# Turning x, q and h into columns with 32x32 turns on VectorE in place of one-column matmuls, in a decode kernel on one core

## The chip, the cores and the metric

One core of one Trainium2 chip. The metric is the device time of one execution in microseconds. It is about 1.8 us longer than the span of the profile, which runs from the first to the last instruction.

Words used below: PE is TensorE, DVE is VectorE, ACT is ScalarE, POOL is GpSimd, SP is the engine that issues the big loads. "big" is the name of the three rotating 8 MB buffers for loads. K0 and V0 are the first pieces of the two caches, K1 and V1 the next. "w12" is w1 and w2 in one load. psq and psh are the accumulators of the matmuls with wq and with w3, and stand for these stages; ps is that of w12, and psB gathers the row that is returned. xT is x as a column, hT the same of h. A "turn" is VectorE's transpose of each 32x32 block. "fetch" is a transfer of a block of instructions. Times of DMA packets count from the same zero as the timelines, the first instruction of the program.

## The reference, cut to what matters

```python
xn = layernorm(x)                                # x: 1 x 1024
q  = xn @ wq                                     # 32 heads of 128
o  = softmax(q @ k_cache.T * 128**-0.5) @ v_cache  # 4 kv heads, 65536 keys: 134 MB of cache
a  = o @ wo
h  = gelu(layernorm(x1) @ w3) @ w4               # x1: the residual of the small mixer w1, w2
return x + a + mlp                               # 1 x 1024
```

One token is decoded, so nearly all of the work is to read the caches and the weights once: 170 MB.

## The kernel before

The loads go through three buffers. A load is issued when the buffer three loads earlier has been released, and a release is the end of the compute on it:

```python
stream = ["wq", "w3", "w12"]
for u in range(NU): stream += [("K", u), ("V", u)]     # wo ahead of the last V, w4 at the end
def pump(self):
    while self.next < len(stream) and self.held < SLOTS:   # SLOTS = 3
        self.load(...)
def done(self, it): self.held -= 1; self.pump()
```

The three places where a row has to become a column, each done with one-column matmuls (cuts marked):

```python
x_row = ogpool.tile([1, D], BF16, ...)
nc.scalar.dma_start(out=x_row[:], in_=A_x[0, 0:1, :])
...
for c in range(DC):                               # x: 8 matmuls
    nc.tensor.matmul(px[:, c:c + 1], lhsT=x_row[0:1, c::DC], rhs=pick4[0:1, 0:1], ...)
...
def row_matmul(acc, rep, cols, n_slices):         # q and h: slices of 512 columns, 4 in
    for c in range(DC):                           # parallel in 4 column groups of PE
        for i in range(2):
            for q in range((n_slices + 1 - i) // 2):
                nc.tensor.matmul(acc[32*q:32*q+32, i, :], lhsT=rep[:, c, :], rhs=cols(c, 2*q+i), ...)
...
for h in range(8):                                # q: 8 matmuls; h: 8 more like them
    nc.tensor.matmul(pq[:, 4, :]..., lhsT=q_row[:, h // 4, ...], rhs=pick4[:], ...)
```

The four column groups hold 32 equal rows each, since the left operand repeats one vector 32 times.

Of the kernel before, what the change touches and what calls it, by code (L numbers as in the profile page):

```python
# [8 lines left out]
BF16 = mybir.dt.bfloat16  # L9
F32 = mybir.dt.float32  # L10
ACTF = mybir.ActivationFunctionType
# [4 lines left out]
P = 128  # L16
# [36 lines left out]
def kernel(  # L53
# [14 lines left out]
    nc = tc.nc  # L68
    nc.at_finalize(keep_loaded_weights)
    D = A_x.shape[-1]  # L70
    S = A_x.shape[1]
    HKV = A_k_cache.shape[1]
# [4 lines left out]
    DC = D // P  # L77
    FC = F // P
# [8 lines left out]
    const = ctx.enter_context(tc.tile_pool(name="const", bufs=1))  # L87
    small = ctx.enter_context(tc.tile_pool(name="small", bufs=1))
    big = ctx.enter_context(tc.tile_pool(name="big", bufs=SLOTS))
    ppool = ctx.enter_context(tc.tile_pool(name="psb", bufs=1))  # L90
    ogpool = ctx.enter_context(tc.tile_pool(name="og", bufs=2))
    ps_S = ctx.enter_context(tc.tile_pool(name="psS", bufs=1, space=bass.MemoryType.PSUM))
    ps_O = ctx.enter_context(tc.tile_pool(name="psO", bufs=1, space=bass.MemoryType.PSUM))
    ps_M = ctx.enter_context(tc.tile_pool(name="psM", bufs=2, space=bass.MemoryType.PSUM))
# [53 lines left out]

    st = Stream()

    x_row = ogpool.tile([1, D], BF16, name="x_row", tag="og")
    nc.scalar.dma_start(out=x_row[:], in_=A_x[0, 0:1, :])
    st.pump()

    ident_f = const.tile([P, P], F32, name="ident_f")
# [4 lines left out]
    nc.gpsimd.memset(ones_f[:], 1.0)  # L160
    warm_act = const.tile([P, 1], F32, name="warm_act")
    nc.scalar.activation(out=warm_act[:], in_=eps_t[:], func=ACTF.Sqrt)
    pick4 = const.tile([P, 4], BF16, name="pick4")
    nc.gpsimd.tensor_copy(out=pick4[:], in_=ident_f[:, ::32])

    spread = ogpool.tile([P, 4, P], BF16, name="spread", tag="og")
    for b in range(2):
        nc.gpsimd.tensor_copy(
            out=spread[:, 2 * b:2 * b + 2, :].rearrange("p r (a i) -> p r a i", a=4),
            in_=ident_f[:, 64 * b:64 * b + 64].rearrange("p (i r) -> p r i", r=2).unsqueeze(2).to_broadcast([P, 2, 4, 32]))  # L170
# [9 lines left out]
        nc.tensor.matmul(psB[32 * j:32 * j + lhsT.shape[1], :], lhsT=lhsT, rhs=rhs, start=start, stop=False,  # L180
                         tile_position=(0, 32 * j), skip_group_check=True)

    px = ps_M.tile([P, 512], F32, name="pm_x", tag="pm")
    for c in range(DC):
        nc.tensor.matmul(px[:, c:c + 1], lhsT=x_row[0:1, c::DC], rhs=pick4[0:1, 0:1], start=True, stop=True)
    xT = const.tile([P, DC], F32, name="xT")
    nc.vector.tensor_copy(out=xT[:], in_=px[:, 0:DC])

    def layernorm(src, tag):
        rowsum = const.tile([P, 1], F32, name=f"ln_rowsum_{tag}", tag="ln_rowsum")  # L190
# [22 lines left out]
    xn, xn_rep, negmean1, rstd1 = layernorm(xT, "a")  # L213
    _, xn2_rep, _, _ = layernorm(xn, "b")
# [14 lines left out]
                          in_=sel8[:].unsqueeze(2).to_broadcast([P, 8, 16]))  # L229

    ln_s1 = const.tile([P, 1], F32, name="ln_s1")
    nc.vector.tensor_scalar(out=ln_s1[:], in0=rstd1[:], scalar1=1.0, scalar2=None, op0=ALU.add)
    ln_s2 = const.tile([P, 1], F32, name="ln_s2")
    nc.vector.tensor_tensor(out=ln_s2[:], in0=negmean1[:], in1=rstd1[:], op=ALU.mult)
    accx = ppool.tile([1, D], F32, name="accx", tag="p")
    nc.vector.tensor_scalar(out=accx[:], in0=x_row[:], scalar1=ln_s1[0:1, 0:1], scalar2=ln_s2[0:1, 0:1],
                            op0=ALU.mult, op1=ALU.add)
    for j in range(2):
        row_acc(j, ident_f[0:1, 0:32], accx[0:1, 512 * j:512 * (j + 1)], start=True)

    def row_matmul(acc, rep, cols, n_slices):
        for c in range(DC):
            for i in range(2):
                for q in range((n_slices + 1 - i) // 2):
                    nc.tensor.matmul(acc[32 * q:32 * q + 32, i, :], lhsT=rep[:, c, :], rhs=cols(c, 2 * q + i),  # L245
                                     start=(c == 0), stop=(c == DC - 1),
                                     tile_position=(0, 32 * q), skip_group_check=True)

    qx = const.tile([P, 4, 8 * HKV], BF16, name="qx")

    def compute_wq():
        wt = st.tiles["wq"][:].rearrange("p (c n) -> p c n", c=DC)
        psq = ps_S.tile([P, SUBS, 512], F32, name="psq", tag="sc")
        row_matmul(psq, xn_rep, lambda c, s: wt[:, c, 512 * s:512 * (s + 1)], 8)
        st.done("wq")
        q_row = ppool.tile([P, 2, 512], BF16, name="q_row", tag="p")
        nc.vector.tensor_copy(out=q_row[:, 0, :], in_=psq[:, 0, :])  # L257
        nc.scalar.copy(out=q_row[:, 1, :], in_=psq[:, 1, :])
        pq = ps_M.tile([P, 5, 8 * HKV], F32, name="pm_q", tag="pm")
        for h in range(8):  # L260
            nc.tensor.matmul(pq[:, 4, :].rearrange("p (g h) -> p g h", h=8)[:, :, h],
                             lhsT=q_row[:, h // 4, P * (h % 4):P * (h % 4 + 1)], rhs=pick4[:], start=True, stop=True)
        qT = small.tile([P, 8 * HKV], BF16, name="qT")
        nc.vector.tensor_copy(out=qT[:], in_=pq[:, 4, :])
        for x in range(4):
            nc.tensor.matmul(pq[:, x, :], lhsT=spread[:, x, :], rhs=qT[:], start=True, stop=True)
        nc.vector.tensor_copy(out=qx[:], in_=pq[:, 0:4, :])

    def place_queries(g):
        for a in range(4):  # L270
# [5 lines left out]
    hT = const.tile([P, FC], BF16, name="hT")  # L276

    def compute_w3():
        wt = st.tiles["w3"][:, 0:DC * F].rearrange("p (c m k) -> p c k m", c=DC, k=FC)
        psh = ps_S.tile([P, SUBS, 512], F32, name="psh", tag="sc")  # L280
        row_matmul(psh, xn2_rep, lambda c, s: wt[:, c, 4 * s:4 * s + 4, :], 7)
        st.done("w3")
        h_rows = ppool.tile([P, 2, 512], BF16, name="h_rows", tag="p")
        nc.vector.memset(h_rows[96:128, 1, :], 0.0)
        nc.scalar.activation(out=h_rows[:, 0, :], in_=psh[:, 0, :], func=ACTF.Gelu_apprx_tanh)
        nc.scalar.activation(out=h_rows[0:96, 1, :], in_=psh[0:96, 1, :], func=ACTF.Gelu_apprx_tanh)
        ph = ps_M.tile([P, 8, 4], F32, name="pm_h", tag="pm")
        for ik in range(8):
            nc.tensor.matmul(ph[:, ik, :], lhsT=h_rows[:, ik // 4, P * (ik % 4):P * (ik % 4 + 1)], rhs=pick4[:],  # L289
                             start=True, stop=True)  # L290
        nc.vector.tensor_copy(out=hT[:, 0:24].rearrange("p (q ik) -> p ik q", q=3), in_=ph[:, :, 0:3])  # L291
        nc.vector.tensor_copy(out=hT[:, 24:28], in_=ph[:, 0:4, 3])

    def compute_w12():
        wt = st.tiles["w12"][:, 0:2 * DC * D].rearrange("p (w c n) -> p w c n", w=2, c=DC)
# [130 lines left out]
    def compute_w4(lo, hi):  # L426
        wt = st.tiles["w4"]
        for c in range(lo, hi):
            for j in range(2):
                row_acc(j, hT[:, c:c + 1], wt[:, D * c + 512 * j:D * c + 512 * (j + 1)])  # L430

    compute_wq()
    compute_w3()
    compute_w12()
    for u in range(NU - 1):
# [4 lines left out]
    for g in range(HKV - 1):  # L440
# [11 lines left out]
                        in_=out_t[:].rearrange("(a b) n -> a b n", b=32)[:, 0, :])  # L452
# [29 lines left out]
```

## Time and profile before

| | before |
|---|---|
| time, median of the first 3 runs | 402.9 us (402.86 to 404.4) |
| span of the profiled run | 402.5 us |
| moved over the span | 170.03 MB, mean 422 GB/s |
| PE, DVE busy | 59%, 51% |

The profiled run is 404.32 us (from result.json of the run).

From the page of the kernel before: engine, busy microseconds, share of the span; the load totals; the instruction queue with its packets, megabytes and share; the chain of waits by engine.

```profile
span 402.5 us, 2599 instructions
PE 235.8 (59%) x1364; PEld 45.9 (11%) x878; DVE 204.7 (51%) x150; ACT 27.4 (7%) x35; POOL 5.5 (1%) x29
...
DMA packets 4576, 170.03 MB, mean 422 GB/s; under 512 B 467, under 2 KB 469, under 8 KB 982
...
q8 instruction: 9, 0.15, 0.1%
...
DMA 47%; PE 22%; DVE 14%; ACT 2%; issue 1%; DVEq 0%; ACTq 0%
```

The chain of waits gives PE and DVE over a third of the span. It would be a mistake to take that as what they cost. The chain walks back from one event to what released it, and a load that was released late still had other loads ahead of it in the queue. The timeline shows that. Its columns are start, duration, engine and line, operation, output and input, count, and in brackets the idle time before it and what ended it.

```profile
0.73 0.37 SPq L128 DMA_DIRECT2D big<-in_A_wq_dram  x1
0.74 0.53 ACTq L152 DMA_DIRECT2D x_row<-in_A_x_dram  x1
...
2.30 0.66 PE L185 MATMUL pm_x<-pick,x_row 1*128 1x1 bf16 x8 [2.30 <-DMA x_row<-in_A_x_dram]
...
22.64 5.39 PE L245 MATMUL psq<-big,ln_rep_a 128*32 128x512 bf16 x64 [11.09 <-DMA big<-in_A_wq_dram]
...
28.07 0.33 SPq L147 DMA_DIRECT2D big<-in_A_k_cache_dram  x1
...
39.57 14.17 PE L245 MATMUL psh<-big,ln_rep_b 128*32 128x512 bf16 x56 [9.34 <-DMA big<-in_B_w_dram]
...
53.77 0.33 SPq L147 DMA_DIRECT2D big<-in_A_v_cache_dram  x1
...
63.50 0.33 SPq L147 DMA_DIRECT2D big<-in_A_k_cache_dram  x1
...
70.28 8.77 DVE L322 STREAM_TRANSPOSE big<-big 128x4096 f32<-128x4096 f32 x2 [13.48 <-DMA big<-in_A_k_cache_dram]
...
396.23 0.99 PE L180 MATMUL psB<-big,hT 128*1 128x512 bf16 x6 [0.44 <-DMA big<-in_B_w_dram]
398.99 0.38 PE L180 MATMUL psB<-big,hT 128*1 128x512 bf16 x2 [1.76 <-DMA big<-in_B_w_dram]
```

K0 is issued at 28.07 while w3 and w12 are still under way. V0 is issued at 53.77 and K0 lands only at 70.28. So the queue always holds something, and what happens between 2 and 64 us should be free to come many microseconds later before a DMA engine is idle.

### The profile page before, as it was taken

What the parts mean: (1) busy time and instruction counts of PE and PEld (TensorE: products, weight loads), DVE (VectorE), ACT (ScalarE), POOL (GpSimd) and SP (SyncE); (2) the same over time, 40 slices, a digit from 0 to 9 for tenths busy, and PEclk for the clock granted to TensorE, in tenths of its full rate; (3) what the DMA queues carried; (4) which work ended last, traced back from release to release, by engine and by line L of the source; (5) the groups of instructions that cost most, each with busy time, mean ns of one, the idle gap of its engine ahead of it and who ended that gap; (6) DMA issues with size and microseconds to landing.
All of it is one profiled execution on the core that took longest, in us unless ns stands there. A gap on an engine that the chain in (4) does not pass through costs nothing.

```text
span 402.5 us, 2599 instructions
## 1 busy us (share of the span) xinstructions
PE 235.8 (59%) x1364; PEld 45.9 (11%) x878; DVE 204.7 (51%) x150; ACT 27.4 (7%) x35; POOL 5.5 (1%) x29
## 2 busy tenths in 40 slices
PE   5160973591579238743975195439354925694983
PEld 2010110000100110010002010100020102010220
DVE  3010000974196569634953895279449750965040
ACT  1000021003000200020002000200200020002000
POOL 2000000000000000000000000000000000000000
PEclk9996888696769787956795689669875976598999
DMA  9989999999999999999999999999999998999893
GB/s 397 436 382 421 443 423 462 469 417 417 418 423 462 462 406 423 417 436 451 456 417 417 430 438 430 469 417 417 423 444 423 469 423 378 430 457 449 381 417 142
DMA packets 4576, 170.03 MB, mean 422 GB/s; under 512 B 467, under 2 KB 469, under 8 KB 982
## 3 DMA queue, kind: packets, MB, share of 16 engines
q1 hardware_dynamic: 4560, 169.87, 98.0%
q8 instruction: 9, 0.15, 0.1%
q10 hardware_dynamic: 6, 0.00, 0.0%
q14 instruction: 1, 0.01, 0.0%
HBM read 169.87 MB, written 0.00 MB: 422 GB/s over the span
## 4 chain that ended last, share of the span: by engine, by line
DMA 47%; PE 22%; DVE 14%; ACT 2%; issue 1%; DVEq 0%; ACTq 0%
DMA big<-in_A_k_cache_dram 32%; PE sc L327 13%; DMA big<-in_A_v_cache_dram 10%; DVE big L322 8%; PE oacc L377 6%; DMA big<-in_B_w_dram 5%; DVE p_sb L348 2%; DVE mx L332 2%; ACT p_sb L345 2%; PE ps L299 1%; PE psB L180 1%; DVE m L336 0%; PE pm_mx L334 0%; DVE ol L397 0%; PE pm_mx L341 0%
## 5 line engine op out<-in xcount | busy, mean ns | idle before, releaser
L327 PE MATMUL sc<-big,qdiag 128*128 128x512 bf16 x512 | 130.5, 417 | 60.3 <-DVE big L322 54.8
L322 DVE STREAM_TRANSPOSE big<-big 128x4096 f32<-128x4096 f32 x32 | 139.4, 4413 | 48.1 <-DMA big<-in_A_k_cache_dram 48.1
L377 PE MATMUL oacc<-big,p_sb 128*32 128x512 bf16 x512 | 42.9, 509 | 34.5 <-DVE p_sb L348 34.5
L332 DVE TENSOR_REDUCE mx<-sc 128x1 f32<-128x2048 f32 x8 | 18.3, 2292 | 30.5 <-PE sc L327 30.5
L327 PEld LDWEIGHTS <-qdiag 128*128 128x128 bf16 x128 | 13.3, 104 | 173.1 <-issue 141.7
L345 ACT ACTIVATE p_sb<-sc,nball 128x2048 bf16<-128x2048 f32 x8 | 15.7, 1967 | 219.6 <-DVE nball L343 219.6
L348 DVE STREAM_TRANSPOSE p_sb<-p_sb 128x2048 bf16<-128x2048 bf16 x8 | 18.5, 2311 | 18.0 <-ACT p_sb L345 18.0
L377 PEld LDWEIGHTS <-p_sb 128*32 128x32 bf16 x512 | 16.3, 123 | 58.5 <-DVE p_sb L348 35.1
L245 PE MATMUL psh<-big,ln_rep_b 128*32 128x512 bf16 x56 | 14.2, 1050 | 9.3 <-DMA big<-in_B_w_dram 9.3
L291 DVE CAST hT<-pm_h 128x24 bf16<-128x24 f32 x1 | 0.3, 265 | 25.9 <-PE pm_h L289 25.9
L334 PE MATMUL pm_mx<-ident_f,mx 128*1 128x128 f32 x8 | 2.2, 270 | 19.1 <-DVE mx L332 19.1
L416 PE MATMUL o_acc<-big,oT 128*1 128x512 bf16 x48 | 11.9, 412 | 2.4 <-ACT p_sb L345 2.4
L245 PE MATMUL psq<-big,ln_rep_a 128*32 128x512 bf16 x64 | 5.4, 511 | 11.1 <-DMA big<-in_A_wq_dram 11.1
L386 DVE SCALAR_TENSOR_TENSOR og<-oacc,wb,og 128x512 f32<-128x512 f32 x4 | 3.0, 746 | 15.4 <-PE oacc L377 15.4
L180 PE MATMUL psB<-big,hT 128*1 128x512 bf16 x56 | 7.4, 378 | 3.7 <-DMA big<-in_B_w_dram 3.7
L257 DVE CAST q_row<-psq 128x512 bf16<-128x512 f32 x1 | 0.7, 692 | 17.2 <-PE psq L245 17.2
L422 DVE COPY o_rows<-o_acc 1x1024 f32<-1x1024 f32 x1 | 1.2, 1212 | 12.9 <-PE oacc L377 12.9
L272 POOL COPY qdiag<-qx 32x32 bf16<-32x32 bf16 x16 | 3.3, 204 | 279.9 <-PE sc L327 251.3
L398 PE MATMUL pm_e<-ol,sel8big 128*128 128x129 f32 x8 | 2.3, 370 | 8.2 <-DVE ol L397 8.2
L299 PE MATMUL ps<-big,ln_rep_b 128*32 128x512 bf16 x16 | 5.3, 507 | 0.0
L341 PE MATMUL pm_mx<-ident_f,rep 1*128 1x1 f32 x8 | 1.9, 234 | 5.0 <-DVE rep L338 5.0
L383 ACT COPY og<-oacc 128x512 f32<-128x512 f32 x4 | 2.3, 586 | 32.7 <-PE oacc L377 32.7
(101 smaller groups left out, 69.6 us busy)
## 6 DMA issues: line engine op xcount, KB each, us to landing
big<-in_A_wo_dram SPq DMA_DIRECT2D x1, 8192.0 KB, 36.8
big<-in_B_w_dram SPq DMA_DIRECT2D x1, 7168.0 KB, 38.4
big<-in_B_w_dram SPq DMA_DIRECT2D x2, 2048.0 KB, 46.5
big<-in_B_w_dram SPq DMA_DIRECT2D x2, 1536.0 KB
big<-in_B_w_dram SPq DMA_DIRECT2D x1, 1280.0 KB, 24.1
big<-in_B_w_dram SPq DMA_DIRECT2D x1, 1024.0 KB, 29.4
big<-in_B_w_dram SPq DMA_DIRECT2D x1, 768.0 KB, 30.8
big<-in_B_w_dram SPq DMA_DIRECT2D x1, 512.0 KB, 31.6
```

The costliest lines, as they stand in the source:

```text
L180: nc.tensor.matmul(psB[32 * j:32 * j + lhsT.shape[1], :], lhsT=lhsT, rhs=rhs, start=start, stop=False, tile_position=(0, 32 * j), skip_gro ...
L245: nc.tensor.matmul(acc[32 * q:32 * q + 32, i, :], lhsT=rep[:, c, :], rhs=cols(c, 2 * q + i), start=(c == 0), stop=(c == DC - 1), tile_posi ...
L272: nc.gpsimd.tensor_copy(out=qdiag[at, LEAD:].rearrange("p (x c) -> p x c", x=4)[:, :, 32 * a:32 * a + 8], in_=qx[at, :, 8 * g:8 * g + 8])
L299: nc.tensor.matmul(ps1[0:32, q, :], lhsT=xn2_rep[:, c, :], rhs=wt[:, 0, c, 512 * q:512 * (q + 1)], start=(c == 0), stop=(c == DC - 1), til ...
L322: nc.vector.transpose(out=words, in_=words)
L327: nc.tensor.matmul(sc[:, e, :], lhsT=qdiag[:, c0:c0 + P], rhs=cols[:, s, e, :, b2, :, r], start=(s == 0 and b2 == 0 and r == 0), stop=(s = ...
L332: nc.vector.reduce_max(out=mx[:], in_=sc[:].rearrange("p e n -> p (e n)"), axis=AX.X)
L345: nc.scalar.activation(out=p_sb[:], in_=sc[:], func=ACTF.Exp, bias=nball[:, b:b + 1], scale=SCALE, accum_out=group["lall"][:, b:b + 1])
L348: nc.vector.transpose(out=flat, in_=flat)
L377: nc.tensor.matmul(oacc[32 * q:32 * (q + 1), :], lhsT=pT[:, e, 32 * t:32 * (t + 1)], rhs=vt[:, :, e, t, :], start=(e == 0 and t < 4), stop ...
L386: nc.vector.scalar_tensor_tensor(out=og[:], in0=oacc[:], scalar=wb[:, 1:2], in1=og[:], op0=ALU.mult, op1=ALU.add)
L416: nc.tensor.matmul(tail["rows"][0:1, h2, :], lhsT=oT[g][:, j:j + 1], rhs=wt[:, g, j, 512 * h2:512 * (h2 + 1)], start=(g == 0 and j == 0), ...
```

## The change

The intent is to take the small matmuls off PE. Each slice of q and h now fills its column group so that column 32a+i of every head lies in column group a. Then one turn of the 32x32 blocks puts each value on its partition. x is loaded into row 0 of a tile of 32 rows that is filled with zeros first, and four turns make it a column.

```diff
-    x_row = ogpool.tile([1, D], BF16, name="x_row", tag="og")
-    nc.scalar.dma_start(out=x_row[:], in_=A_x[0, 0:1, :])
+    x_row = ogpool.tile([32, D], BF16, name="x_row", tag="og")
+    nc.vector.memset(x_row[:], 0.0)
+    nc.scalar.dma_start(out=x_row[0:1, :], in_=A_x[0, 0:1, :])
...
-    for c in range(DC):
-        nc.tensor.matmul(px[:, c:c + 1], lhsT=x_row[0:1, c::DC], rhs=pick4[0:1, 0:1], start=True, stop=True)
+    for a in range(4):
+        nc.vector.transpose(out=x_t[32 * a:32 * a + 32].rearrange("p c j -> p (c j)"),
+                            in_=x_row[:, 256 * a:256 * (a + 1)].rearrange("p (i c) -> p c i", c=DC))
...  (row_matmul takes widths: q 512 + 512, h 512 + 384 columns in each of 4 groups)
-        row_matmul(psq, xn_rep, lambda c, s: wt[:, c, 512 * s:512 * (s + 1)], 8)
+        row_matmul(psq, xn_rep, lambda c, i, a: wt[:, c, 16 * i:16 * (i + 1), a, :], (512, 512))
...  (the 8 matmuls for q and the copy to qT go)
+        flat = q_row[:].rearrange("p i n -> p (i n)")
+        nc.vector.transpose(out=flat, in_=flat)
...
-        row_matmul(psh, xn2_rep, lambda c, s: wt[:, c, 4 * s:4 * s + 4, :], 7)
+        row_matmul(psh, xn2_rep, lambda c, i, a: wt[:, c, 16 * i:min(16 * (i + 1), FC), 32 * a:32 * (a + 1)],
+                   (512, 32 * FC - 512))
...  (the 8 matmuls for h, a fill and two copies go)
+        nc.vector.transpose(out=h_row[:], in_=h_row[:])
+        nc.vector.tensor_copy(out=hT[:], in_=h_row[:, ::32])
```

More of the change, by code (lines that the diff above doesn't have):

```diff
@@ L162 @@
     nc.scalar.activation(out=warm_act[:], in_=eps_t[:], func=ACTF.Sqrt)
-    pick4 = const.tile([P, 4], BF16, name="pick4")
-    nc.gpsimd.tensor_copy(out=pick4[:], in_=ident_f[:, ::32])
     spread = ogpool.tile([P, 4, P], BF16, name="spread", tag="og")
@@ L181, in row_acc @@
                          tile_position=(0, 32 * j), skip_group_check=True)
-    px = ps_M.tile([P, 512], F32, name="pm_x", tag="pm")
-    for c in range(DC):
-        nc.tensor.matmul(px[:, c:c + 1], lhsT=x_row[0:1, c::DC], rhs=pick4[0:1, 0:1], start=True, stop=True)
+    x_t = ppool.tile([P, DC, 32], BF16, name="x_t", tag="p")
+    for a in range(4):
+        nc.vector.transpose(out=x_t[32 * a:32 * a + 32].rearrange("p c j -> p (c j)"),
+                            in_=x_row[:, 256 * a:256 * (a + 1)].rearrange("p (i c) -> p c i", c=DC))
     xT = const.tile([P, DC], F32, name="xT")
-    nc.vector.tensor_copy(out=xT[:], in_=px[:, 0:DC])
+    nc.vector.tensor_copy(out=xT[:], in_=x_t[:, :, 0])
     def layernorm(src, tag):
@@ L235 @@
     accx = ppool.tile([1, D], F32, name="accx", tag="p")
-    nc.vector.tensor_scalar(out=accx[:], in0=x_row[:], scalar1=ln_s1[0:1, 0:1], scalar2=ln_s2[0:1, 0:1],
+    nc.vector.tensor_scalar(out=accx[:], in0=x_row[0:1, :], scalar1=ln_s1[0:1, 0:1], scalar2=ln_s2[0:1, 0:1],
                             op0=ALU.mult, op1=ALU.add)
@@ L239, with row_matmul @@
         row_acc(j, ident_f[0:1, 0:32], accx[0:1, 512 * j:512 * (j + 1)], start=True)
-    def row_matmul(acc, rep, cols, n_slices):
+    def row_matmul(acc, rep, cols, widths):
         for c in range(DC):
-            for i in range(2):
-                for q in range((n_slices + 1 - i) // 2):
-                    nc.tensor.matmul(acc[32 * q:32 * q + 32, i, :], lhsT=rep[:, c, :], rhs=cols(c, 2 * q + i),
+            for i, n in enumerate(widths):
+                for q in range(4):
+                    nc.tensor.matmul(acc[32 * q:32 * q + 32, i, 0:n], lhsT=rep[:, c, :], rhs=cols(c, i, q),
                                      start=(c == 0), stop=(c == DC - 1),
@@ L251, in compute_wq @@
     def compute_wq():
-        wt = st.tiles["wq"][:].rearrange("p (c n) -> p c n", c=DC)
+        wt = st.tiles["wq"][:].rearrange("p (c h a i) -> p c h a i", c=DC, a=4, i=32)
         psq = ps_S.tile([P, SUBS, 512], F32, name="psq", tag="sc")
-        row_matmul(psq, xn_rep, lambda c, s: wt[:, c, 512 * s:512 * (s + 1)], 8)
+        row_matmul(psq, xn_rep, lambda c, i, a: wt[:, c, 16 * i:16 * (i + 1), a, :], (512, 512))
         st.done("wq")
@@ L258, in compute_wq @@
         nc.scalar.copy(out=q_row[:, 1, :], in_=psq[:, 1, :])
-        pq = ps_M.tile([P, 5, 8 * HKV], F32, name="pm_q", tag="pm")
-        for h in range(8):
-            nc.tensor.matmul(pq[:, 4, :].rearrange("p (g h) -> p g h", h=8)[:, :, h],
-                             lhsT=q_row[:, h // 4, P * (h % 4):P * (h % 4 + 1)], rhs=pick4[:], start=True, stop=True)
-        qT = small.tile([P, 8 * HKV], BF16, name="qT")
-        nc.vector.tensor_copy(out=qT[:], in_=pq[:, 4, :])
+        flat = q_row[:].rearrange("p i n -> p (i n)")
+        nc.vector.transpose(out=flat, in_=flat)
+        pq = ps_M.tile([P, 4, 8 * HKV], F32, name="pm_q", tag="pm")
         for x in range(4):
-            nc.tensor.matmul(pq[:, x, :], lhsT=spread[:, x, :], rhs=qT[:], start=True, stop=True)
-        nc.vector.tensor_copy(out=qx[:], in_=pq[:, 0:4, :])
+            nc.tensor.matmul(pq[:, x, :], lhsT=spread[:, x, :], rhs=flat[:, ::32], start=True, stop=True)
+        nc.vector.tensor_copy(out=qx[:], in_=pq[:])
     def place_queries(g):
@@ L280, in compute_w3 @@
         psh = ps_S.tile([P, SUBS, 512], F32, name="psh", tag="sc")
-        row_matmul(psh, xn2_rep, lambda c, s: wt[:, c, 4 * s:4 * s + 4, :], 7)
+        row_matmul(psh, xn2_rep, lambda c, i, a: wt[:, c, 16 * i:min(16 * (i + 1), FC), 32 * a:32 * (a + 1)],
+                   (512, 32 * FC - 512))
         st.done("w3")
-        h_rows = ppool.tile([P, 2, 512], BF16, name="h_rows", tag="p")
-        nc.vector.memset(h_rows[96:128, 1, :], 0.0)
-        nc.scalar.activation(out=h_rows[:, 0, :], in_=psh[:, 0, :], func=ACTF.Gelu_apprx_tanh)
-        nc.scalar.activation(out=h_rows[0:96, 1, :], in_=psh[0:96, 1, :], func=ACTF.Gelu_apprx_tanh)
-        ph = ps_M.tile([P, 8, 4], F32, name="pm_h", tag="pm")
-        for ik in range(8):
-            nc.tensor.matmul(ph[:, ik, :], lhsT=h_rows[:, ik // 4, P * (ik % 4):P * (ik % 4 + 1)], rhs=pick4[:],
-                             start=True, stop=True)
-        nc.vector.tensor_copy(out=hT[:, 0:24].rearrange("p (q ik) -> p ik q", q=3), in_=ph[:, :, 0:3])
-        nc.vector.tensor_copy(out=hT[:, 24:28], in_=ph[:, 0:4, 3])
+        h_row = ppool.tile([P, 32 * FC], BF16, name="h_row", tag="p")
+        nc.scalar.activation(out=h_row[:, 0:512], in_=psh[:, 0, :], func=ACTF.Gelu_apprx_tanh)
+        nc.scalar.activation(out=h_row[:, 512:], in_=psh[:, 1, 0:32 * FC - 512], func=ACTF.Gelu_apprx_tanh)
+        nc.vector.transpose(out=h_row[:], in_=h_row[:])
+        nc.vector.tensor_copy(out=hT[:], in_=h_row[:, ::32])
     def compute_w12():
```

## The prediction

> **What bounds the kernel.** Transfers. The page's DMA line gives 170.03 MB at 422 GB/s over the 402.5 us span; the stretch table a DMA share of 1.00 up to 395 us. PE is busy 59%, DVE 51%. The chain of waits names DMA for 47% and PE and DVE for 36%, but three big buffers keep transfers queued: in SP's timeline V0 is issued at 53.8 us while K0 lands only at 70.3 and V1 at 91.4, 17.5 us before K1 lands. The queue never runs dry, so work after a landing is hidden unless it is late by more than about 16 us. Exposed: 1 us before the first load, 3.5 us after the last landing at 398.9.
>
> **What the change touches.** All of it lies before 64 us (timeline).
> - x: removes 8 one-column matmuls (0.66 us). Adds a 32x1024 fill (estimate 0.5 us, from the 0.27 us fill of half its columns), which holds back x's load, and four 32x256 turns. The trace's turns take 2.31 us for 2048 bf16 columns and 4.40 for 4096 words: 0.1 us fixed and 1.1 ns a column, so 0.4 us each. xT is ready at about 4.5 to 5 us instead of 3.2, both layernorms at about 12.5 instead of 10.9. wq lands at 22.6: hidden, 10 us to spare.
> - q: removes 8 matmuls and a 0.19 us copy; adds a 128x1024 turn, estimate 1.2 us. Queries ready 0.5 to 1 us later than 30.6; K0's matmuls need them at 74.8.
> - h: removes 8 matmuls, a fill (0.27) and one of two copies; adds a 128x896 turn, estimate 1.05 us. hT is needed only at 386 us.
> - wq columns: now runs of 32 (64 bytes). 64 matmuls as before, 5.4 us, unchanged: the Trainium skill, "SBUF — State Buffer" (section on the partition-to-port map, note on cachelines) says full bandwidth wants consecutive accesses to the same 16-byte line; these runs have them.
> - w3 columns keep their 56-byte step, every access in another line; the trace agrees with the note: groups of concurrent matmuls follow each other every 0.875 us, against 0.21 us for wq's late groups, and groups of 3 take as long as groups of 4. So the cost goes by columns per group: 2 x 512 becomes 512 + 384. 14.2 us becomes 12.4. V0 is issued about 1.8 us earlier, w12 is done about 2 us earlier than 63.5.
>
> **On the critical path:** none. K0 still lands near 70.3, where the transposes start. An earlier release only lengthens the queue. The tail is untouched.
>
> **Predicted: 403.0 us, range 401.8 to 404.7.** The width is run-to-run spread: before's runs are 402.86, 402.9 and 404.4. Faster by over 2%: 1%; within 2%: 98%; slower by over 2%: 1%.
>
> **What the profile would show.** Right: mean GB/s within 1% of 422; K0's first transpose within 0.5 us of 70.3; psh 12.4 us; psq within 1 us of 5.4; the x turns under 0.5 us each; V0's issue near 52. Wrong: psh still near 14.2 (then the columns read in total count, not those per group); psq well above 6.5 us (64-byte runs cost); x's turns far above 0.5 us (their 16-byte step costs); K0 landing moved.
>
> **What would make it wrong.** The removed small tiles shift the big buffers' addresses by some tens of bytes; if transfers care, all 400 us scale. A hidden stage over 16 us later: psq or psh at more than twice its time. Or x's load, now behind a fill, waiting behind the big loads for many us: more than 10 us would delay wq's release.

## The result, and the profile after

After: 402.8 us median of 6 runs (402.68 to 402.85). Before, in the same rounds: 403.6 us (402.86 to 404.4). The ratio of fast runs is 0.9979, with a 95% interval of 0.9961 to 0.9997. Ratios here are the mean time of one kernel's fast runs over that of the other's of the same rounds, so not quite the ratio of the medians.

The interval stays below 1, and the reason is visible in the runs: the kernel before has two times. Three of its six runs are at 402.9 and three near 404.3. The kernel after has only the lower one. All of these runs are fast, and the clock does not tell the two times apart: in the 33 later runs of before with a clock on record it is 0.795 to 0.817 in the short ones and 0.794 to 0.813 in the long ones. That gap of 1.4 us is not in the prediction, and most of the experiments went to it.

The same lines from the page of the kernel after:

```profile
span 400.9 us, 2563 instructions
PE 230.4 (57%) x1348; PEld 44.2 (11%) x854; DVE 209.0 (52%) x154; ACT 27.3 (7%) x35; POOL 5.3 (1%) x28
...
DMA packets 4575, 170.01 MB, mean 424 GB/s; under 512 B 467, under 2 KB 469, under 8 KB 982
...
q8 instruction: 8, 0.13, 0.1%
...
DMA 52%; DVE 26%; PE 16%; ACT 3%; another core or an unknown queue 2%; issue 1%; DVEq 0%; ACTq 0%
```

DVE's share of the chain went from 14% to 26% while its busy time rose by 4 us and the kernel did not get slower. That is one more reason not to read such shares as costs. The timeline of the kernel after:

```profile
0.73 0.37 SPq L128 DMA_DIRECT2D big<-in_A_wq_dram  x1
...
1.41 0.52 ACTq L153 DMA_DIRECT2D x_row<-in_A_x_dram  x1
...
10.25 2.50 DVE L184 STREAM_TRANSPOSE x_t<-x_row 32x256 bf16<-32x256 bf16 x4 [8.87 <-DMA x_row<-in_A_x_dram]
...
22.83 5.87 PE L245 MATMUL psq<-big,ln_rep_a 128*32 128x512 bf16 x64 [1.30 <-DMA big<-in_A_wq_dram]
...
28.73 0.33 SPq L147 DMA_DIRECT2D big<-in_A_k_cache_dram  x1
...
39.74 12.41 PE L245 MATMUL psh<-big,ln_rep_b 128*32 128x512 bf16 x64 [7.98 <-DMA big<-in_B_w_dram]
...
52.19 0.33 SPq L147 DMA_DIRECT2D big<-in_A_v_cache_dram  x1
...
58.60 0.33 SPq L147 DMA_DIRECT2D big<-in_A_k_cache_dram  x1
...
70.15 8.77 DVE L315 STREAM_TRANSPOSE big<-big 128x4096 f32<-128x4096 f32 x2 [15.61 <-DMA big<-in_A_k_cache_dram]
...
396.07 1.02 PE L179 MATMUL psB<-big,hT 128*1 128x512 bf16 x6 [0.46 <-DMA big<-in_B_w_dram]
397.36 0.38 PE L179 MATMUL psB<-big,hT 128*1 128x512 bf16 x2 [0.26 <-DMA big<-in_B_w_dram]
```

Three readings. V0 and K1 are issued 1.6 and 4.9 us earlier, and K0 still lands at the same place (70.15 against 70.28). x is there 8 us later than before (10.25 against 2.30), so that psq waited only 1.30 us for wq where PE had waited 11.09. And the end differs: up to 396 us the two kernels are within 0.2 us of each other, then before waits 1.76 us for the last piece of w4 and after waits 0.26.

The packets that start between 396.8 and 398.6 us of the kernel before show what that last piece waited for (queue, start, end, bytes; queue 8 fetches instructions, queue 1 is the big loads; read from the trace's list of packets):

```
q8  396.80  397.91  16384
q1  396.81  396.82      4
q1  396.81  396.91   2048
q1  396.90  396.91      4
q1  397.90  398.13   2048
q1  398.12  398.34   2048
q1  398.33  398.35      4    (the completion of the last piece)
```

The Trainium skill, "Runtime: NRT & Kernel Launch" (section Instruction fetch mechanics), says that an engine's sequencer fetches its program in blocks of 16 KiB, 256 instructions, over a DMA queue, and that the cost is mostly hidden. The trace agrees on the size: packets of 16,384 bytes, nine in before, eight in after, 1.0 to 1.1 us each. The pages count 2242 matmuls and weight loads on PE in before and 2202 in after, 40 fewer. (The expectations speak of 1705 and 1665 "listed" instructions. That listing is 537 below the pages' count in every run of the table further down, so its differences are the same.)

The theories for the missing 1.4 us:
- A: a fetch that falls beside the last loads holds one DMA engine up; 40 instructions less on PE moved it off the end.
- B: the gain is the work saved and the earlier releases.
- C: the removed small tiles shift the addresses of the big buffers.

### The profile page after: what moved, and what is told of

The parts are those of the page before. It is cut to its first block, busy times and chain, and to the rows that moved or that the text cites. A ratio compares the mean times of both kernels' runs of the same rounds, so it can differ in the third digit from the quotient of the medians.

```text
span 400.9 us, 2563 instructions
## 1 busy us (share of the span) xinstructions
PE 230.4 (57%) x1348; PEld 44.2 (11%) x854; DVE 209.0 (52%) x154; ACT 27.3 (7%) x35; POOL 5.3 (1%) x28
## 4 chain that ended last, share of the span: by engine, by line
DMA 52%; DVE 26%; PE 16%; ACT 3%; another core or an unknown queue 2%; issue 1%; DVEq 0%; ACTq 0%
DMA big<-in_A_k_cache_dram 31%; DVE big L315 19%; DMA big<-in_A_v_cache_dram 10%; PE sc L320 8%; PE oacc L370 6%; DMA big<-in_A_wq_dram 6%; DMA big<-in_B_w_dram 4%; DVE p_sb L341 3%; DVE mx L325 3%; ACT p_sb L338 3%; PE psq L245 1%; PE pm_mx L327 0%; DVE m L329 0%; PE pm_mx L334 0%
## 5 line engine op out<-in xcount | busy, mean ns | idle before, releaser
L320 PE MATMUL sc<-big,qdiag 128*128 128x512 bf16 x512 | 127.7, 409 | 66.4 <-DVE big L315 66.4
L370 PE MATMUL oacc<-big,p_sb 128*32 128x512 bf16 x512 | 44.7, 521 | 34.5 <-DVE p_sb L341 34.5
L245 PE MATMUL psh<-big,ln_rep_b 128*32 128x512 bf16 (+1 forms) x64 | 12.4, 941 | 8.0 <-DMA big<-in_B_w_dram 8.0
L409 PE MATMUL o_acc<-big,oT 128*1 128x512 bf16 x48 | 12.5, 428 | 2.4 <-ACT p_sb L338 2.4
L284 DVE STREAM_TRANSPOSE h_row<-h_row 128x896 bf16<-128x896 bf16 x1 | 1.1, 1111 | 21.1 <-ACT h_row L283 21.1
L184 DVE STREAM_TRANSPOSE x_t<-x_row 32x256 bf16<-32x256 bf16 x4 | 2.5, 616 | 8.9 <-DMA x_row<-in_A_x_dram 8.9
```

Of the source, the lines that this page charges most:

```text
L184: nc.vector.transpose(out=x_t[32 * a:32 * a + 32].rearrange("p c j -> p (c j)"), in_=x_row[:, 256 * a:256 * (a + 1)].rearrange("p (i c) -> ...
L245: nc.tensor.matmul(acc[32 * q:32 * q + 32, i, 0:n], lhsT=rep[:, c, :], rhs=cols(c, i, q), start=(c == 0), stop=(c == DC - 1), tile_positio ...
L320: nc.tensor.matmul(sc[:, e, :], lhsT=qdiag[:, c0:c0 + P], rhs=cols[:, s, e, :, b2, :, r], start=(s == 0 and b2 == 0 and r == 0), stop=(s = ...
L370: nc.tensor.matmul(oacc[32 * q:32 * (q + 1), :], lhsT=pT[:, e, 32 * t:32 * (t + 1)], rhs=vt[:, :, e, t, :], start=(e == 0 and t < 4), stop ...
L409: nc.tensor.matmul(tail["rows"][0:1, h2, :], lhsT=oT[g][:, j:j + 1], rhs=wt[:, g, j, 512 * h2:512 * (h2 + 1)], start=(g == 0 and j == 0), ...
```

## The experiments

All kernels but two compute the right result by their indices. The kernel before was run beside each group: over all rounds it has 39 runs, 15 from 402.69 to 403.22 and 24 from 404.04 to 404.64.

### 1. After, with PE's program made as long as before's

```diff
+    pm_pad = ps_M.tile([P, 512], F32, name="pm_pad", tag="pm")
+    for i in range(20):
+        nc.tensor.matmul(pm_pad[:, i:i + 1], lhsT=spread[:, i % 4, :], rhs=g_col[:], start=True, stop=True)
```

> The kernel after, with 20 idle one-column matmuls and their 20 weight loads put at the head of TensorE's program (done by about 7 us, nothing waits for them), so that TensorE's program is again as long as before's: 1705 listed instructions against 1665. Theory A (the last 1.4 us of before's slower runs is one 16 KB instruction fetch that the length of TensorE's program puts beside the last w4 pieces): the page counts 9 instruction packets instead of 8, one of them near 396 to 397 us, and the times split in two again, part near 402.8 and part near 404.2. Rival B (the gain comes from less work and earlier releases before 64 us): head as in after, so all runs stay near 402.8. Rival C (shifted buffer addresses): the same, all near 402.8.

Measured: 404.21 us median, one run of six at 402.92 and five from 404.06 to 404.46. The idle matmuls ran from 2.75 to 3.43 us; V0 was issued at 51.97, as early as in after. The ninth fetch is back, at 396.74 us. The count of the queue on the page of this run:

```profile
q8 instruction: 9, 0.15, 0.1%
```

and the end of its timeline:

```profile
396.21 1.04 PE L179 MATMUL psB<-big,hT 128*1 128x512 bf16 x6 [0.44 <-DMA big<-in_B_w_dram]
398.93 0.38 PE L179 MATMUL psB<-big,hT 128*1 128x512 bf16 x2 [1.68 <-DMA big<-in_B_w_dram]
```

This kernel has after's early releases and adds no tile to the buffers' memory (its one new tile is in the matmul accumulators), and it has before's times. B and C fall.

### 2. Before, with the same 40 instructions added

The same edit on the kernel before.

> The kernel before with the same 20 matmuls and 20 loads added: 1745 listed TensorE instructions against 1705. Theory A: the ninth fetch comes 40 instructions earlier, some microseconds ahead of the end, while every DMA engine still has data queued, so all runs are near 402.8 and none near 404.3, although the kernel does more. Rivals B and C: nothing of before's head or addresses is taken away, so the times stay split, 402.9 and 404.3, or are a little longer.

Measured: 404.22 us, all six runs from 403.99 to 404.90. The ninth fetch moved to 392.97 us as expected, but the times went all to the long side, not to the short one. A's claim that a fetch some microseconds ahead of the end does no harm was wrong.

### 3. Only the x part; 4. only the q and h parts

Number 3 is the kernel before with the first two hunks of the diff; number 4 is the kernel after without them.

> Only the x part of the change. TensorE's program is 16 instructions shorter than before's. Theory A: 8 instruction packets, all runs near 402.8. Rival B: this part only makes the head later (x lands near 10 us instead of 2.3), so the times stay split as before's. Both: x's load lands near 10 us, its four turns take about 0.6 us each, psq starts near 22.8, no other time lost.

> Only the q and h parts; x by matmuls and its load as before. TensorE's program is 24 instructions shorter than before's. Theory A: 8 instruction packets, all runs near 402.8. Rival B: this part holds the earlier releases (psh 12.4 us, V0 issued near 52), so it alone should hold all of the gain, near 402.8 as well. Both: x's load lands near 2.3 us, psh 12.4 us.

Measured: x part 403.18 us (402.89 to 404.73), the q and h parts 402.80 (402.70 to 404.26). Both pages count eight fetches, and all twelve spans are 400.9 to 401.2, as after's. x's turns start at 10.28 in number 3; its psh is 14.2 us and V0 is issued at 53.86. In number 4 x's column starts at 2.15 from its matmuls, and V0 and K1 are issued at 51.96 and 58.37. So each part alone has the short span, the one with the earlier releases and the one without.

The spans are short but some times are not (404.26 with a span of 401.0). In the profiled runs of these two kernels the trace shows a ninth fetch after the span has ended. In number 4 it lies at 403.26 to 404.49 us and that run took 404.26, 3.3 over its span. In number 3 it lies at 401.61 to 403.00 and the run took 402.98, 1.8 over its span, as runs without such a fetch do. So an execution could be over only when this fetch is, and be long when it comes late; with two runs traced, that is a reading and not shown.

### 5. Before, with 160 instructions added

```diff
+    for i in range(80):
+        nc.tensor.matmul(pm_pad[:, i:i + 1], lhsT=spread[:, i % 4, :], rhs=g_col[:], start=True, stop=True)
     compute_wq()
```

> The kernel before with 80 idle matmuls and their 80 loads put ahead of the wq stage: 1865 listed TensorE instructions against 1705. Theory A: the ninth fetch moves 160 instructions ahead, to about 384 us, where the kernel after had its last one without harm, and a tenth is not reached. So nine instruction packets, the last near 384, all spans 400.9 to 401.3 and all times near 402.8, although the kernel does more than before. Rivals B (earlier releases) and C (addresses): nothing is gained, times split as before's (402.8 and 404.3) or all near 404.2 as in the second run, whose 40 instructions are a part of these.

Measured: 404.05 us, all six from 403.83 to 404.22. The ninth fetch is at 385.06 us. In after the eighth, at 383.44, does no harm. So it is not the distance from the end. The completions of each load on the 16 DMA engines point to what it is. Below, for five loads: the time of the first engine's completion, and how many microseconds behind it each of the 16 came, sorted (worked out from the trace):

```
after, V0 and the last V:
  86.97  0.00 0.14 0.15 0.16 0.18 0.21 0.22 0.22 0.25 0.28 0.30 0.31 0.34 0.37 0.77 1.97
 377.50  0.00 0.12 0.12 0.18 0.21 0.27 0.32 0.74 1.11 1.65 1.72 1.75 1.79 1.81 1.89 1.94
after, the piece of w4 after its fetch at 383.44:
 384.28  0.00 0.12 0.12 0.18 0.21 0.27 0.74 1.11 1.64 1.71 1.74 1.78 1.81 1.87 1.88 1.94
before with 160 more, ahead of its ninth fetch at 385.06 and after it:
 381.15  0.00 0.02 0.17 0.22 0.30 0.48 0.59 1.37 1.57 1.75 1.80 1.81 1.92 1.98 2.01 2.14
 384.24  0.00 0.02 0.16 0.21 0.30 0.48 0.58 1.37 1.57 1.75 1.79 1.80 1.92 2.00 2.13 3.52
```

Each fetch makes one engine late by 1.1 to 1.6 us, and the engine stays late from load to load. In after the fetches strike engines that were early (0.32 became 1.87 or 1.88), so the largest lag stays near 1.9 while the number of late engines grows. The ninth fetch of the padded kernel strikes an engine that was late already: all the early lags are still in the list, and one of about 2.0 has become 3.52. The trace does not name the engine of a packet, so which one is struck is read from these lists. From here theory A2: the first eight fetches fall on different engines and the last completion hardly moves; the ninth falls on one that was struck before and moves it by about 1.3 us.

### 9. After, with 500 instructions added: ten fetches, far from the end

The edit of number 1 with 250 in place of 20.

> The kernel after with 250 idle matmuls and their 250 loads at the head: 2165 listed TensorE instructions against 1665, so ten fetches inside the stream, the ninth near 335 us and the tenth near 377, both far from the end. Theory A2, formed after the fifth run (each fetch makes one of the 16 DMA engines about 1.1 us late for good; the first eight fall on eight different engines, the ninth and tenth on engines that are late already): the end is set by engines hit twice, so every run is about 1.3 us over the kernel after: spans 402.1 to 402.9, times near 404.1, as with nine fetches. Rival A (only a fetch in the last few microseconds costs): spans near 401, times 402.8. Rival D (every fetch more costs 1.3 us): 2.6 us over, near 405.4.

Measured: 404.14 us, all six from 404.06 to 404.42, spans 402.3 to 402.6. The ninth fetch came at 338.00, the tenth at 385.67 (expected near 377). At the load that completes from 338.59 on the largest lag is 3.38 us and at 377.51 it is 3.41, so it lasts for 39 us; after the tenth fetch two engines are at 3.26 and 3.36. The fetches on this run's page and the end of its timeline:

```profile
q8 instruction: 10, 0.16, 0.2%
...
397.52 1.05 PE L179 MATMUL psB<-big,hT 128*1 128x512 bf16 x6 [0.22 <-DMA big<-in_B_w_dram]
398.82 0.38 PE L179 MATMUL psB<-big,hT 128*1 128x512 bf16 x2 [0.26 <-DMA big<-in_B_w_dram]
```

The time is one step up, not two, and the step does not depend on the distance from the end. A and D fall, and A2 holds. The last packets agree with it: no fetch is near them in numbers 2, 5 and 9, and still 2 KB packets follow one another, every 0.08 us, to 398.0, 398.4 and 398.3 us, as a single row in numbers 2 and 5 and as two in number 9, where after's last one ends at 396.86.

| kernel | PE matmuls and weight loads | ninth fetch, us | spans, us |
|---|---|---|---|
| after | 2202 | none | 400.9 to 401.1 |
| 4, q and h only | 2218 | 403.26, after the span | 400.9 to 401.0 |
| 3, x only | 2226 | 401.61, after the span | 401.0 to 401.2 |
| before, all groups | 2242 | 396.80 | 12 runs 400.9 to 401.4, 21 runs 402.3 to 402.9 |
| 1, after and 40 | 2242 | 396.74 | one 401.1, five 402.3 to 402.7 |
| 2, before and 40 | 2282 | 392.97 | 402.1 to 403.1 |
| 5, before and 160 | 2402 | 385.06 | 402.1 to 402.4 |
| 9, after and 500 | 2702 | 338.00 | 402.3 to 402.6 |

(Of the six runs of before that went with after only the times are known; they divide three to three.) At 2242 the fetch starts 0.1 us before the other engines' last packets end, which would explain two times: sometimes the engine has finished by then. No short run of before was traced, so that stays a reading. Which engine a fetch goes to is not settled either, nor why the lags draw together to 0.9 or 1.0 us in the small pieces near the end of every trace read for this and open again, to 2.2 and 2.4 us, at the very last one in numbers 9 and 5.

### 6. After, with x loaded into 32 rows at once

```diff
-    nc.vector.memset(x_row[:], 0.0)
-    nc.scalar.dma_start(out=x_row[0:1, :], in_=A_x[0, 0:1, :])
+    nc.scalar.dma_start(out=x_row[:], in_=A_x[0, 0:1, :].to_broadcast([32, D]))
```

> The kernel after, with x loaded into all 32 rows at once instead of into one row after a fill, so that its load waits for nothing and is issued at about 0.73 us, before the big loads' first packets at about 2. Theory: x lands near 2.5 us instead of 10, because it no longer stands behind whole 64 KB packets; both layernorms end near 13 instead of 20.8. Time unchanged, 402.8 within 0.3: this wait was hidden. Rival (the fill and the turns are what makes x late): x ready still near 10.

Measured: x was issued at 0.73 and still its turns start at 10.81, so the expectation missed. The packets tell why. In before x was one packet, on its DMA engine at 1.67 us, ahead of the first packets of wq at 1.74 (the expectation of number 10 says 1.91, counted from 0.24 us before the timeline's zero). Here each engine has two packets of x and a completion. The first of each go at 4.74, 7.24 and 9.80: one after each 64 KB packet of wq, which take 2.42 us each once they are under way. In after the one packet, issued 0.7 us later than in before, goes at 7.34 and its completion at 9.83. The Trainium skill, "DMA: Bandwidth & Descriptors" (section Queues, rings and completion order), says that an engine goes round its queues packet by packet; the trace agrees, and with 64 KB packets one round is 2.42 us. The rival was no better: without the fill, and before any turn, x landed as late.

The time is 403.15 us (403.05 to 403.34), 0.35 us over after's median, and the last V completes at 377.91 to 379.82 us on the 16 engines, against 377.50 to 379.44 in after. After was not run again in this group, where before's short times are 402.69 to 403.03, so the size is uncertain. The later V fits that the extra packets at the head of the stream were not absorbed: a delay of the stream itself would count, unlike a delay of the compute. No run isolates it.

### 10. After, with x loaded into a tile of its own and copied

```diff
+    x_one = ppool.tile([1, D], BF16, name="x_one", tag="p")
+    nc.scalar.dma_start(out=x_one[:], in_=A_x[0, 0:1, :])
     nc.vector.memset(x_row[:], 0.0)
-    nc.scalar.dma_start(out=x_row[0:1, :], in_=A_x[0, 0:1, :])
+    nc.vector.tensor_copy(out=x_row[0:1, :], in_=x_one[:])
```

> The kernel after, with x loaded into a one-row tile of its own at once (one packet, issued near 0.73 us as in before) and copied by VectorE into row 0 of the filled 32 rows. Theory (the single packet issued early gets ahead of the first 64 KB packets, as before's did at 1.91; 32 packets did not): x lands near 2.3 us, the turns start near 3.1 to 3.5, both layernorms end near 14 instead of 20.8. Time as the kernel after, 402.8 within 0.3. Rival: the load's place does not matter, turns start near 10 again.

Measured: 402.75 us (402.66 to 402.81). The timeline of this run:

```profile
2.13 0.47 DVE L155 COPY x_row<-x_one 1x1024 bf16<-1x1024 bf16 x1 [0.75 <-DMA x_one<-in_A_x_dram]
2.63 2.51 DVE L186 STREAM_TRANSPOSE x_t<-x_row 32x256 bf16<-32x256 bf16 x4
```

x's packet went at 1.64 us, and the second layernorm ended at 13.1 in place of 20.8. One copy of 0.47 us buys back 7.7 us of slack. It buys no time, because that slack was not used up: the best version is as fast as after, not faster.

### 7 and 8. After, with the head held back by turns

```diff
+    for _ in range(36):          # 76 in number 8
+        held = x_t[:].rearrange("p c j -> p (c j)")
+        nc.vector.transpose(out=held, in_=held)
     xT = const.tile([P, DC], F32, name="xT")
```

> The kernel after, with 36 turns of x's columns in place on VectorE ahead of the layernorm (an even count puts them back; about 0.38 us each, 14 us). psq then starts near 36 us and ends near 41, K0 is issued near 41 to 42 instead of 28.7. Theory (a release is hidden until the queue runs dry, and w12 lands near 48.6): time unchanged, 402.8 within 0.4. Rival (the head is on the critical path): 14 us longer.

> The same with 76 turns, about 29 us. psq ends near 56 to 57 us, K0 is issued then, 6 to 9 us after w12 has landed near 48.6 to 50.5, and its first packets follow about 1.3 us later. Theory: 7 to 10 us longer than the kernel after, 410 to 413. Rival (all of the head counts): 29 us longer. Rival (none of it counts): 402.8.

Measured: number 7 held the column of x back by 17.3 us (each turn took 0.48 us and not 0.38), K0 was issued at 44.77 in place of 28.73, and the time is 403.01 (402.97 to 403.10): 0.2 over after, with a median inside the short times of before in the same group. Number 8 held it back by 36.5 us; K0 was issued at 64.49:

```profile
64.49 0.33 SPq L147 DMA_DIRECT2D big<-in_A_k_cache_dram  x1
```

and here the queue ran dry. From the table by stretches of this run (microseconds; PE, PEld, DVE, ACT, POOL busy; clock; DMA share; GB/s):

```profile
50.00:60.00 10.00, 8.13 (x33) 2.90 (x29) 3.32 (x18) 0.52 (x2) 0.00 (x0) 1.00 0.00 0
```

420.59 us (420.35 to 420.93), 17.8 over after. The expectation of 410 to 413 missed because the delay was longer than reckoned. In the form of the theory it fits: K0 was issued 35.8 us later than in after, 17.7 us of span were lost, and 18.1 us were absorbed. No packet of a load moved from 49.41 to 65.45 us, so 16.0 of the 17.7 us are seen directly as an idle queue. So K0's release is free for the 16 us of number 7, and up to about 18 if it costs one for one beyond that, which one run past the limit cannot show.

### 11. After, without the 32 turns of K

```diff
-            words = t[:, W * s:W * (s + 1)].bitcast(F32)
-            nc.vector.transpose(out=words, in_=words)
```

> The kernel after without the 32 turns of K on VectorE; the result is wrong on purpose. VectorE's busy time falls by 139 us, from 209 to about 70. Theory (the stream of transfers binds, VectorE is hidden): 402.8 within 0.4. Rival (the chain of waits means what it says: VectorE is 26% of the span, 104 us): much faster, 300 to 390.

The page of this run:

```profile
PE 231.1 (58%) x1348; PEld 44.3 (11%) x854; DVE 69.8 (17%) x122; ACT 27.3 (7%) x35; POOL 5.3 (1%) x28
...
DMA 67%; PE 24%; DVE 5%; ACT 2%; issue 1%; ACTq 0%
```

Measured: 403.32 us, runs of 402.84, 402.93, 403.71 and 404.04. VectorE lost 139 us of work and nothing got faster: 0.5 us over after's median, a little outside the expected 0.4. Eight fetches were traced in its profiled run, a short one. Why two of the four were longer, with spans of 401.9 and 402.2, is open. The comparison with the reference passed this kernel, although it computes attention from unturned keys, and it passed the next one too: its tolerance does not reach these parts of the answer, so the layout of the change was checked by its indices instead; no run shows it.

### 12. After, with two reads made dense

```diff
-  x: in_=x_row[:, 256 * a:256 * (a + 1)].rearrange("p (i c) -> p c i", c=DC)
+  x: in_=x_row[:, 256 * a:256 * (a + 1)]
-  w3: .rearrange("p (c m k) -> p c k m", c=DC, k=FC)
+  w3: .rearrange("p (c k m) -> p c k m", c=DC, k=FC)
```

> The kernel after with two reads made dense, the result wrong on purpose: w3's columns are read in order instead of 56 bytes apart, and x's turns read their 256 columns in order instead of 16 bytes apart. Theory (the distance between consecutive reads costs): psh falls from 12.4 us to 5 to 6, x's turns from 0.62 to about 0.4 us each. Rival (four column groups and turns on 32 rows cost that much anyway): 12.4 and 0.62 stay. Time 402.8 within 0.4 under both, since both stages are hidden.

Groups of the kernel after by shape, columns: engine, operation, output and input, shapes, count, busy us, mean ns of one, idle before.

```profile
L245 PE MATMUL psh<-big,ln_rep_b 128*32 128x512 bf16 x32 | 8.5, 1047 | 8.0 <-DMA big<-in_B_w_dram 8.0
L245 PE MATMUL psh<-big,ln_rep_b 128*32 128x384 bf16 x32 | 6.8, 835 | 0.0
L184 DVE STREAM_TRANSPOSE x_t<-x_row 32x256 bf16<-32x256 bf16 x4 | 2.5, 616 | 8.9 <-DMA x_row<-in_A_x_dram 8.9
```

The same of this run:

```profile
L245 PE MATMUL psh<-big,ln_rep_b 128*32 128x512 bf16 x32 | 4.2, 516 | 8.8 <-DMA big<-in_B_w_dram 8.8
L245 PE MATMUL psh<-big,ln_rep_b 128*32 128x384 bf16 x32 | 3.5, 427 | 0.0
L184 DVE STREAM_TRANSPOSE x_t<-x_row 32x256 bf16<-32x256 bf16 x4 | 1.7, 436 | 9.0 <-DMA x_row<-in_A_x_dram 9.0
```

The busy times of the two shapes overlap. The stage as a whole goes from 12.41 us to 4.8 (from 39.47 to V0's issue at 44.26), a little under the expected 5 to 6. The turns go from 616 to 436 ns. The clock does not explain it: the groups of 512 columns in after take 0.87 us where the record reads 0.50 (up to 44.5 us) and 0.87 us where it reads 1.00, while the dense ones take 0.42 and then 0.22. So in these two reads the distance between elements is what costs. V0 is issued 7.9 us earlier than in after, and the one run, of unknown state, took 402.71 us: nothing gained, as it should be.

## Why the prediction was right or wrong, point by point

- **Transfers bind, and the change lies off the critical path: right, and shown.** With 139 us of VectorE's work gone the time stays (number 11); a head 17 us later costs 0.2 us (number 7); one 36 us later costs 17.8 (number 8). The figure of "about 16 us" of cover was worked out for V0's release; the runs tested K0's, which measured about 18.
- **403.0 us, range 401.8 to 404.7: right** (402.8). But "the width is run-to-run spread" was a wrong account of before's 402.86 and 404.4. They are two outcomes, 1.4 us apart, and the change removed one. The range held because it was taken from both outcomes, not because their cause was seen: that part is luck. The term missing from the sum was the length of PE's program: 40 instructions fewer, so the ninth fetch is not reached inside the stream (numbers 1, 2, 5 and 9).
- **psh 14.2 to 12.4, cost by columns per group: right**, 12.41. V0's issue "near 52": 52.19.
- **psq unchanged with runs of 64 bytes: right within its bound**, 5.87 against 5.39, and the 0.5 us is not the layout. In both kernels groups of four matmuls follow each other every 0.42 to 0.43 us at first and every 0.21 us from the moment at which the trace's clock record begins, with 1.00: 26.2 us in before, 27.4 in after. Over the 13 runs with an unbroken psq stage its length, 5.1 to 6.5 us, follows that moment, 3.0 to 5.8 us after its start, in both layouts. This fits the note on cachelines of the Trainium skill, "SBUF — State Buffer" (section on the partition-to-port map), by which accesses that stay in a 16-byte line go at full bandwidth and each one that crosses to another line pays: the runs of 64 bytes show no cost, and the step of 56 bytes does (number 12).
- **x's turns 0.4 us: wrong**, 0.616. The step that failed is "0.1 us fixed and 1.1 ns a column", taken from dense reads. The read every 16 bytes adds 0.18 us (number 12).
- **xT ready at 4.5 to 5, layernorms at 12.5: wrong**, 12.96 and 20.84. The prediction counted the fill's 0.5 us and named the wait behind the big loads only as a risk. It came: 8 us for 2 KB. By PE's idle time before psq, another 1.3 us would have begun to delay it.
- **q ready 0.5 to 1 us later, turns of 1.2 and 1.05 us: about right.** Turns 1.25 and 1.11 us; queries at 32.1 against 30.6, of which 0.7 is psq's later end.
- **w12 done about 2 us earlier: too little**, 4.9. Beside psh's 1.8 us, a table load of 1.28 us that stood between psh and the gelu now ran at 31.4 us, and PE, idle for 1 us and not 2 at that place, ran the first 13 matmuls of w12 in 2.96 us and not 4.67. The granted clock there was 1.00; in before it was 0.50 from 57.0 to 60.4 us. Worth nothing here.

## What to carry to other kernels

When loads are queued ahead, read the slack from the time between a load's issue and the landing of the one before it, not from the shares of the chain of waits; here it was about 18 us, and compute that moved inside it was free in both directions. A kernel that is bound by transfers still notices what goes through the same DMA engines: a 2 KB load issued after the big ones waits for whole packets, and each block of instructions fetched made one engine late. If a kernel has two times a microsecond apart, look for the packets of other queues among the last ones before calling it noise.

## What the Trainium skill lacked or had wrong

- "Runtime: NRT & Kernel Launch", Instruction fetch mechanics, calls a block's fetch mostly hidden. Here a fetch of 16,384 bytes took 1.0 to 1.1 us of one DMA engine, an engine stayed 1.1 to 1.6 us late through the loads of K and V, and the ninth fetch cost 1.3 to 1.4 us of the kernel's time.
- The same page does not say that a fetch can follow the last instruction: at 403.26 us in a span of 401.0, with a time of 404.26.
- "DMA: Bandwidth & Descriptors", Queues, rings and completion order, tells of turns by packets of 9 to 17 descriptors. It gives no time for one: a packet of 64 KB took 2.42 us here, and a 2 KB load with its completion landed 8 us later behind such packets.
- "SBUF — State Buffer" gives no size for the cost of another line at each read: groups of four matmuls of 512 columns took 0.87 us each at a step of 56 bytes, against 0.42 and then 0.22 us dense, and the stage of w3 4.8 us dense against 12.4.
- "VectorE: DVE Perf Modes", The three transpose paths, has one time (311 ns for 128x128 bf16) and does not say how the data lie. Turns of 256 bf16 columns on 32 rows took 436 ns dense and 616 ns when read every 16 bytes.
